# The first step of a batched Fourier transform: opposite rows folded by VectorE, products on 32x32 parts of TensorE

## The chip, the cores and the metric

The kernel runs on one core of a Trainium2 chip. The metric is the device time of one execution in microseconds (us). Each stated time is a median over runs; each profile is one execution recorded by the hardware profiler. The engines are called PE (TensorE, with PEld for its weight loads), DVE (VectorE), ACT (ScalarE), POOL (GpSimd) and SP (SyncE, which here only issues DMAs).

## The reference

Input is x with 8 batches of 3008 rows by 256 channels, in fp32. Along the 3008 rows each channel is Fourier transformed, multiplied by a complex filter, and transformed back; then a feed-forward block follows.

```python
X = np.fft.rfft(x, axis=1)
y = np.fft.irfft(X * (filt_r + 1j * filt_i), n=3008, axis=1)
h = y.reshape(8 * 3008, 256)
g = h @ w_gate                       # 256 x 1536
out = (g / (1 + np.exp(-g)) * (h @ w_val)) @ w_out   # 1536 x 256
```

## The kernel before

3008 is 47 x 64. A transform is done in steps of matrix products: the first is a discrete transform of length 47 over the rows that lie 64 apart, and later steps handle the 64 columns. The input is real, so half the spectrum is kept: NS = 24 of the 47 frequencies, each as a cosine and a sine row, 48 rows.

The main loop runs over the 8 batches `b`. In each batch 12 groups follow one another, 4 chunks of rows by 3 parts of the hidden dimension. A group is called a step, and a step takes some 27.6 us of PE when only the feed-forward block and little else is in it. In each step the program walks one list of 174 tokens, SCHEDULE, written by hand. A token names one piece of work: P, Q, A, B, E are products of the feed-forward block, and f, c, x, s, m, e, l, h, v and others are the ACT, DVE and POOL operations that feed them or take their results out of PSUM. Every instruction is put down in the order of this walk on its engine's queue (`pin` keeps it), so an engine never does a later one first.

The transform of batch b+1 is laid into the steps of batch b. The tokens b0 to b7 advance a generator of the step: in steps 0 to 3 `nxt.quads(g)`, the first step of the transform in four parts g, in steps 4 to 10 `nxt.fours(w)`, the later steps. This holds from batch 2's transform on, thus for six transforms; batches 0 and 1 are transformed in another way (`stage1` and on), and the first batch's steps are busy with preparing tables and weights as well.

`quads(g)` takes two pieces u of x. In SBUF a piece is a tile with 47 rows on partitions 0 to 46 (columns n) and 47 on partitions 64 to 110 (columns n + 32), loaded by `load_x` straight from x. At b0 PE makes eight products from these with the table `quad` (47 x 64, of which 48 columns are used), on four 64x64 quarters of its array, into four PSUM banks `wqa`. At b1 and b2 ACT copies the bank of one half and DVE adds and subtracts the bank of the other half. At b3 and b4 ACT's queue stores 48 rows to the DRAM tile `d`, and `load_x(u + 2)` asks for later pieces. At b5 and b6 of part 3 the filter and the first load of `fours`, `load_four(0)`, are asked for.

All SBUF tiles of the transform are rooms in one tile, `lent`, cut into 14 units of 512 floats per partition; `room_of` gives a letter's place (x the four units from 0, y and g two each after them, then e, t and tb). The first two loads of x for a transform, `following.load_x`, stand in step 11 of the batch before it, at tokens Q2 and B01. The weights of the feed-forward block are loaded anew for each step, in four pieces on SP's queue (`reload_weights`).

Names in the profile: `wk`, `wa` and `we` are PSUM banks of the gate and value products of the feed-forward block; `x`, `D`, `f`, `c`, `m` are SBUF operands made from them; `wA`, `wF` and `wG` are banks of the output product and `o` its sum in SBUF. DVE writes some operands into PSUM ahead of the products that add to them: `wa<-wk,f` (L1097), `wa<-wk,D` (L1097) and `we<-wk,c` (L335); PE can't start these products sooner.

Of the kernel before, what the change touches and what calls it, by code (L numbers as in the profile page):

```python
# [69 lines left out]
NV = 2  # L70
# [55 lines left out]
def dft_tables():  # L126
    n1, n2 = np.arange(N1), np.arange(N2)
    s, q = np.arange(NS), np.arange(NQ)
    ph = 2 * np.pi * (np.outer(n1, s) % N1) / N1
    w = np.stack([np.cos(ph), -np.sin(ph)], 1)  # L130
    wf = np.zeros((N1, 2, NS, 2, 2))
    wi = np.zeros((NS, 2, 2, N1, 2))

    v = np.stack([2 * np.cos(ph), -2 * np.sin(ph)], 0)
    v[0, :, 0], v[1, :, 0] = 1.0, 0.0
    for h in range(2):
        wf[:, h, :, :, h] = w.transpose(0, 2, 1)
# [24 lines left out]
    for tile_, first in zip(BACK, BACK_AT):  # L162
        for i, (n, row, a, rows) in enumerate(tile_):
            if n >= NH:
                back[row:row + rows, first + N1 * i:first + N1 * (i + 1)] = one_hi[a:a + rows]

    quad = np.zeros((128, 64))
    for h, turn in enumerate((ph, ph + 2 * np.pi * s / (2 * N1))):
        cols = np.stack([np.cos(turn), -np.sin(turn)], 2).reshape(N1, 2 * NS)
        quad[64 * h:64 * h + N1, 0:2 * NS] = cols  # L170
# [35 lines left out]
def kernel(  # L206
# [60 lines left out]
    def weights_of(b, k, g):  # L267
        return wt_1 if b == 0 and k < NT and g == 1 else wt_t

    dram_tiles = [wdpool.tile([2 * NS, N2, C], FP32, name=f"d{1 + i % 2}_{i // 2}")  # L270
                  for i in range(4)]
    yt_dram = [wdpool.tile([128, 3 * len(PAIRS), TQ], FP32, name=f"yt_{k}") for k in range(NT)]
    y_dram = [wdpool.tile([128, 8, TQ], FP32, name=f"y_{k}") for k in range(NCHUNK)]
    o_dram = [wdpool.tile([128, 4 * NH, RP], FP32, name=f"o_{k}") for k in range(NT)]
# [39 lines left out]

    def negated_filter(w, stage):

        t = room_of("et"[w % 2])[0:64].rearrange("p (s c) -> p s c", c=C)
# [282 lines left out]
    class Spectral:  # L600


        def __init__(self, b):
            self.b = b
            self.d1, self.d2 = [dram_tiles[2 * (b % 2) + i] for i in range(2)]
            self.d1_rows = self.d1.rearrange("a (h n) c -> (a h) n c", h=2)

# [21 lines left out]
        def load_x(self, u):  # L629
# [4 lines left out]
                        self.load(out=x0[u][r, a:a + n, :],  # L634
                                  in_=rows[r, 8 * u + a:8 * u + a + n, :])
            elif self.b > 1:
                if u < N_QUAD:
                    self.x[u] = room_of("x", u).rearrange("p (n c) -> p n c", c=C)
                    rows = x[self.b].rearrange("(r n) c -> r n c", n=N2)
                    for h in range(2):  # L640
                        for a, e in ((0, 32), (32, N1)):
                            self.load(out=self.x[u][64 * h + a:64 * h + e],
                                      in_=rows[a:e, 32 * h + 4 * u:32 * h + 4 * u + 4])
            elif u < N_ONE:
                self.x[u] = xpool.tile([NR, NV, C], FP32, name=f"x_{self.b}_{u}", tag="x")
                rows = x[self.b].rearrange("(r n) c -> r n c", n=32)
# [52 lines left out]
        def bank(self, name):  # L699
# [2 lines left out]
                return bank(name).rearrange("p (i c) -> p i c", i=NV)  # L702
            return fbank(name)

        def quads(self, g):

            pieces = (2 * g, 2 * g + 1)
            banks = {}
            for u in pieces:
                xt = self.x.pop(u)  # L710
                for h in range(2):
                    banks[u, h] = bank(f"qa_{self.b}_{u}_{h}")
                for cp in range(2):
                    for h in range(2):
                        r = slice(64 * h, 64 * h + N1)
                        pin(nc.tensor.matmul(  # L716
                            out=banks[u, h][64 * cp:64 * cp + 64], lhsT=quad_t[0][r, 0:64],
                            rhs=xt[r, 2 * cp:2 * cp + 2].rearrange("p n c -> p (n c)"),
                            start=True, stop=True))
            yield  # L720
            t1 = {u: room_of("yg"[i]).rearrange("p (n h c) -> p n h c", h=2, c=C)
                  for i, u in enumerate(pieces)}
            for u in pieces:
# [5 lines left out]
            d1 = self.d1.rearrange("a (n h) c -> a n h c", h=2)  # L729
            for u in pieces:  # L730
                for cp in range(2):
                    n = 4 * u + 2 * cp
                    pin(nc.scalar.dma_start(out=d1[:, n:n + 2], in_=t1[u][64 * cp:64 * cp + 2 * NS]))
                self.load_x(u + 2)
                yield
            if g == 3:
                self.load_filter(0)
                self.load_turns(0)
            yield
            if g == 3:  # L740
                self.load_four(0)

        def load_four(self, w):

            if w < N_FOUR:
                t = self.t2[w] = room_of("t").rearrange("p (s h c) -> p s h c", h=2, c=C)
                d1 = self.d1.rearrange("(s r) (n h) c -> s (r n) (h c)", r=2, h=2)
                for p in range(2):
                    s = 4 * w + 2 * p
                    self.load(out=t[64 * p:64 * p + 64].rearrange("p s h c -> p s (h c)"),  # L750
                              in_=d1[s:s + 2].rearrange("s q c -> q s c"))

        def load_filter(self, w):

# [626 lines left out]
    for b in range(B):  # L1381
# [10 lines left out]
        if b and nxt:  # L1392
            for n in range(N_QUAD // 2):
                bursts[n] = nxt.quads(n)
            for n in range(N_FOUR + 1):
                bursts[N_QUAD // 2 + n] = nxt.fours(n)
        bursts = [iter(p) for p in bursts]
        two = []
        for u in range(N_TWO + 2) if b == 0 else ():
# [18 lines left out]
        for step in range(NCHUNK * NG + (b == B - 1)):  # L1418
# [16 lines left out]
            for place, token in enumerate(SCHEDULE):  # L1435
# [31 lines left out]
                    continue  # L1467
                if b == 0 and (step, op) == (5, "A23"):
                    nxt.load_two(0)
                if b + 2 < B and (step, op) in ((11, "Q2"), (11, "B01")):  # L1470
                    following.load_x(int(op == "B01"))
                if b == 1 and step < 4 and op in FILTER_AT:
                    n = FILTER_AT.index(op)
                    if n < 4 and step < 3:
# [48 lines left out]
```

## Time and profile before

| | us |
|---|---|
| median of 3 runs (lowest, highest) | 2822.13 (2820.03, 2825.05) |
| profiled execution, its own time | 2823.7 |
| its span in the profile | 2821.6 |
| PE busy in it | 2787.5 |
| a step with `quads` (steps 0 to 2, step 3) | 29.2, 27.6 |
| a step with `fours` | 27.6 |

The mean granted TensorE clock was 0.997. The span runs from the first to the last recorded instruction; the execution's own time has 2.1 us more around it. "Busy" of PE counts matmuls that overlap one another once. An idle time is put beside the instruction that ended it, with the engine that released it.

### The profile page before, as it was taken

The numbers are of one execution on the slowest core, as the hardware profiler recorded it, in microseconds if no ns is written. First come the engines' busy times: TensorE is split into PE (matmuls) and PEld (weight loads), VectorE is DVE, ScalarE is ACT, GpSimd is POOL, SyncE is SP. The second block draws the span as 40 slices with busy tenths as digits, with TensorE's granted clock in tenths as the row PEclk, the third lists the DMA queues.
The fourth block names the chain that finished last, engine by engine and source line by source line (L and its number), as shares of the span: only waits on it lengthen the run. The fifth ranks groups of instructions, "written<-read, shape, count | busy, mean of one in ns | idle before, by whom it ended". The sixth has DMA issues, their size and how long they took to land.

```text
span 2821.6 us, 48540 instructions
## 1 busy us (share of the span) xinstructions
PE 2787.5 (99%) x15444; PEld 2319.9 (82%) x15444; DVE 1999.1 (71%) x4579; ACT 1564.7 (55%) x4176; POOL 1579.9 (56%) x1689
## 2 busy tenths in 40 slices
PE   8999999999999999999999999999999999999998
PEld 6877888888888888788888888878888888888887
DVE  7898767767667766667766677667676767666666
ACT  5675455555555555555555555555555555555554
POOL 4786576465545565456653566445655455545544
PEclk9999999999999999999999999999999999999999
DMA  9687876877666775667666676667766677654443
GB/s 214 224 272 237 283 242 211 285 233 232 181 188 207 246 221 175 204 215 229 222 185 197 211 246 201 188 190 236 228 205 181 213 224 227 192 153 148 153 137 82
DMA packets 362933, 586.59 MB, mean 208 GB/s; under 512 B 198620, under 2 KB 245660, under 8 KB 362536
## 3 DMA queue, kind: packets, MB, share of 16 engines
q1 hardware_dynamic: 337722, 533.61, 60.8%
q10 hardware_dynamic: 22318, 44.38, 5.7%
q0 software_dynamic: 2640, 5.51, 0.7%
q8 instruction: 125, 2.05, 0.3%
q14 instruction: 128, 1.05, 0.1%
HBM read 467.48 MB, written 101.34 MB: 202 GB/s over the span
## 4 chain that ended last, share of the span: by engine, by line
PE 91%; POOL 2%; DVE 2%; DMA 1%; issue 1%; ACT 1%; ACTq 0%; SPq 0%; POOLq 0%; DVEq 0%
PE wa L1075 25%; PE wk L1075 17%; PE wA L1172 16%; PE we L1075 13%; PE wG L1172 8%; PE wF L1172 4%; PE pd L978 3%; PE wqa L716 2%; PE wqc L775 1%; PE wqb L787 1%; POOL out_dram L1157 0%; POOL h L331 0%; PE pa L857 0%; DMA lent<-later_tbl 0%; PE pd L981 0%
## 5 line engine op out<-in xcount | busy, mean ns | idle before, releaser
L1075 PE MATMUL wa<-y_t,wt_t 128*128 128x188 f32 x4464 | 881.6, 324 | 4.0 <-DVE wa L1097 2.3
L1075 PEld LDWEIGHTS wa<-y_t,wt_t 128*128 128x128 f32 x4464 | 749.8, 191 | 79.5 <-ACT wa L1101 9.3
L1075 PEld LDWEIGHTS wk<-y,wt_t 128*128 128x128 f32 x2976 | 495.0, 190 | 109.5 <-issue 33.4
L1075 PE MATMUL wk<-y,wt_t 128*128 128x188 f32 x2976 | 572.0, 325 | 3.2 <-ACT f L1090 3.2
L331 POOL TENSOR_TENSOR h<-h 128x376 f32<-128x376 f32 x572 | 559.6, 1000 | 15.4 <-DVE h L328 15.2
L328 POOL TENSOR_TENSOR h<-h 128x376 f32<-128x376 f32 x190 | 182.8, 983 | 685.5 <-DVE h L1122 685.5
L1172 PE MATMUL wA<-h,wo_t 128*128 128x376 f32 x1532 | 551.8, 482 | 3.9 <-DVE o L328 2.1
L1075 PE MATMUL we<-y_t,wt_t 128*128 128x188 f32 x2232 | 431.7, 323 | 1.6 <-ACT we L1106 1.5
L331 POOL TENSOR_TENSOR D<-f,f 128x376 f32<-128x376 f32 x288 | 280.0, 986 | 258.4 <-ACT f L1090 256.0
L331 DVE TENSOR_TENSOR we<-we,m 128x376 f32<-128x376 f32 x576 | 319.8, 556 | 141.1 <-PE we L1075 73.9
L1075 PEld LDWEIGHTS we<-y_t,wt_t 128*128 128x128 f32 x2232 | 369.3, 190 | 2.7 <-ACT we L1106 2.1
L1172 PEld LDWEIGHTS wA<-h,wo_t 128*128 128x128 f32 x1532 | 274.9, 190 | 113.7 <-issue 7.0
L1110 ACT COPY m<-wa 128x376 f32<-128x376 f32 x576 | 272.7, 473 | 102.0 <-PE wa L1075 98.8
L335 DVE SCALAR_TENSOR_TENSOR y<-wk,c 128x376 f32<-128x376 f32 x480 | 244.8, 541 | 63.8 <-ACT c L1094 37.8
L1117 ACT ACTIVATE g<-wa 128x188 f32<-128x188 f32 x576 | 187.5, 326 | 164.7 <-PE wa L1075 154.9
L1117 ACT ACTIVATE u<-we 128x188 f32<-128x188 f32 x576 | 188.7, 328 | 160.2 <-DVE we L331 153.3
L1172 PE MATMUL wG<-h,wo_t 128*128 128x376 f32 x768 | 274.0, 479 | 0.0
L1094 ACT COPY c<-wk 128x376 f32<-128x376 f32 x288 | 136.5, 474 | 226.0 <-PE wk L1075 196.7
L1090 ACT ACTIVATE f<-wk 128x376 f32<-128x376 f32 x288 | 140.4, 488 | 168.6 <-PE wk L1075 118.0
L1106 ACT COPY we<-y 128x376 f32<-128x376 f32 x480 | 222.3, 480 | 19.8 <-DVE h L1122 14.4
L1122 DVE TENSOR_TENSOR h<-wa,g 128x188 f32<-128x188 f32 x576 | 199.4, 347 | 38.0 <-ACT g L1117 37.6
L1122 DVE TENSOR_TENSOR h<-we,u 128x188 f32<-128x188 f32 x576 | 198.5, 345 | 28.8 <-ACT u L1117 17.3
(193 smaller groups left out, 3523.0 us busy)
## 6 DMA issues: line engine op xcount, KB each, us to landing
wt_t<-w_all SPq DMA_DIRECT2D x174, 896.0 KB
wt_t<-w_all SPq DMA_DIRECT2D x174, 768.0 KB
lent<-filter SPq DMA_DIRECT2D x36, 1024.0 KB
lent<-d SPq DMA_DIRECT2D x84, 256.0 KB
d<-lent ACTq DMA_DIRECT2D x84, 256.0 KB
d<-lent ACTq DMA_DIRECT2D x96, 192.0 KB
lent<-raw SPq DMA_DIRECT2D x144, 128.0 KB
t<-d SPq DMA_DIRECT2D x114, 128.0 KB
```

The lines of the kernel that those rows point to most:

```text
L328: return eng.tensor_tensor(out=dst, in0=a, in1=b, op=ALU.add)
L331: return eng.tensor_tensor(out=dst, in0=a, in1=b, op=ALU.subtract)
L335: return nc.vector.scalar_tensor_tensor(out=dst, in0=a, scalar=-1.0, in1=b, op0=ALU.mult, op1=ALU.subtract)
L978: pin(nc.tensor.matmul(out=rows, lhsT=self.t4[k, i][:, j, ts(cb, 128)], rhs=cols, start=j == 0, stop=True, skip_group_check=True))
L1075: pin(nc.tensor.matmul(out=ps[:, z], lhsT=self.wt[:, SLOT[p], z], rhs=rhs, start=start and z == 0, stop=True, skip_group_check=True))
L1090: pin(act.mul(self.small(f"f{i}", f"f{i}", 1), t[f"k{i}"], -1.0))
L1094: pin(act.copy(out=self.small(f"c{i}", f"c{i}", 1), in_=t[f"k{i}"]))
L1106: pin(act.copy(out=self.bank(f"e{at}"), in_=t[f"y{at}"]))
L1110: pin(act.copy(out=self.small(f"m{at}", "m", 4), in_=t[f"a{at}"]))
L1117: pin(act.activation(out=self.small(op, "g", 3, 1)[:, 0], in_=ps[:, 1], func=AF.Silu))
L1122: pin(v.tensor_tensor(out=dst, in0=ps[:, 0], in1=g, op=ALU.mult))
L1172: pin(nc.tensor.matmul(out=self.tiles[at], lhsT=wo_t[:, JB * q + i, WO[p], :], rhs=self.hs[i][:, HID[p]], start=start and i == 0, stop=Tru ...
```

## The change

Rows a and 47 - a of a discrete transform of length 47 share their cosine and have opposite sines. The changed kernel uses this. `fold(g)` lets DVE add and subtract 128x512 tiles `up` and `down` (four operations for each part g), and the products at b0 are 24 rows by 32 columns, with a cosine table for sums and a sine table for differences: sixteen of them for a part, on sixteen 32x32 parts of PE's array, into the same four banks. A part's pieces are now g and g + 4. The two halves of the frequencies (even and odd turns) stand in separate 32-row blocks, so 64 rows are stored for each piece, unmixed, to a new DRAM tile `quads_dram`.

`down` needs the rows in falling order. `turn_rows`, called in step 8 at token Q0 of the batch two before, copies them from x to the DRAM tile `turned`, with a negative stride, by six DMAs on SP's queue. `load_x(g)` then loads one `down` tile of 128 x 1024 (from `turned`) and four `up` blocks of 32 x 1024. `load_x(0)` stands in step 11 at Q0; `load_x(g + 1)` follows the fold's last operation at b7. `first_fold` does the fold of part 0 at b4 to b7 of step 11; the fold of part g + 1 runs at b4 to b7 of part g's own step. `load_four` reads the new layout by four DMAs in place of two. The table `quad` and the room of `negated_filter` (batch 1 only) are changed to suit.

On each engine this comes to, over the program: PE 192 products of 64x512 replaced by 384 of 32x512; DVE 96 operations added; SP 192 loads of x replaced by 24 and 96, with 36 copies and 72 issues of `load_four` added; ACT 96 stores of 192 KB replaced by 96 of 256 KB.

```diff
+            self.quads_dram, self.turned = quads_dram[b % 2], turned_dram[b % 2]
...
-                if u < N_QUAD:
-                    self.x[u] = room_of("x", u).rearrange("p (n c) -> p n c", c=C)
+                if u < N_QUAD // 2:
+                    self.x[u] = [room_of("x", n) for n in range(2)]
+                    up, down = self.x[u]
+                    at = self.turned.rearrange("(g q) p c -> g p q c", q=4)[u]
+                    self.load(out=down.rearrange("p (q c) -> p q c", c=C), in_=at)
                     rows = x[self.b].rearrange("(r n) c -> r n c", n=N2)
-                    for h in range(2):
-                        for a, e in ((0, 32), (32, N1)):
-                            self.load(out=self.x[u][64 * h + a:64 * h + e],
-                                      in_=rows[a:e, 32 * h + 4 * u:32 * h + 4 * u + 4])
+                    for n in range(4):
+                        first = 16 * n + 4 * u
+                        self.load(out=up[ts(n, 32)].rearrange("p (q c) -> p q c", c=C),
+                                  in_=rows[0:32, first:first + 4])
...
+        def turn_rows(self):
+            xb, to = x[self.b], self.turned
+            end = NS if self.b > 3 else 32
+            for h in range(2):
+                for i in range(2):
+                    n, p = 32 * h + 16 * i, 1 - h
+                    lane = 64 * h + 32 * i
+                    self.load(out=to[:, lane + p:lane + end],
+                              in_=bass.AP(tensor=xb.tensor, ap=[[C, 16], [-N2 * C, end - p], [1, C]],
+                                          offset=xb.offset + ((N1 - 1) * N2 + n) * C))
+                    if h == 0:
+                        self.load(out=to[:, lane], in_=xb[n:n + 16])
+
+        def fold(self, g):
+            if g < N_QUAD // 2:
+                up, down = self.x.pop(g)
+                self.x[g] = [room_of("e"), room_of("t")]
+                for t, f in zip(self.x[g], (add, sub)):
+                    for half in range(2):
+                        a = ts(half, NV * C)
+                        pin(f(nc.vector, t[:, a], up[:, a], down[:, a]))
+                        if t is self.x[g][1] and half:
+                            self.load_x(g + 1)
+                        yield
+
+        def first_fold(self):
+            for _ in range(4):
+                yield
+            yield from self.fold(0)
+
         def quads(self, g):
-            pieces = (2 * g, 2 * g + 1)
...
+            pieces = (g, g + N_QUAD // 2)
+            banks = {(u, h): bank(f"qa_{self.b}_{u}_{h}") for u in pieces for h in range(2)}
+            parts = self.x.pop(g)
+            for cp in range(2):
+                for t in range(2):
+                    for i, u in enumerate(pieces):
+                        for h in range(2):
+                            r, c = 32 * (2 * h + i), 32 * (2 * cp + t)
+                            pin(nc.tensor.matmul(
+                                out=banks[u, h][c:c + 32], lhsT=quad_t[0][r:r + NS, ts(t, 32)],
+                                rhs=parts[t][r:r + NS, ts(cp, NV * C)],
+                                start=True, stop=True))
+            yield
+            fold = self.fold(g + 1)
...
-                    pin(nc.scalar.dma_start(out=d1[:, n:n + 2], in_=t1[u][64 * cp:64 * cp + 2 * NS]))
-                self.load_x(u + 2)
+                    pin(nc.scalar.dma_start(out=d1[:, n:n + 2], in_=t1[u][64 * cp:64 * cp + 64]))
+                if u == pieces[1]:
+                    next(fold, None)
                 yield
             if g == 3:
                 self.load_filter(0)
                 self.load_turns(0)
+            next(fold, None)
             yield
             if g == 3:
                 self.load_four(0)
+            next(fold, None)
+            yield
+            next(fold, None)
...
-                    self.load(out=t[64 * p:64 * p + 64].rearrange("p s h c -> p s (h c)"),
-                              in_=d1[s:s + 2].rearrange("s q c -> q s c"))
+                    for r in range(2):
+                        a = 64 * p + 32 * r
+                        self.load(out=t[a:a + 32].rearrange("p s h c -> p s (h c)"),
+                                  in_=d1[r, :, s:s + 2])
...
+        if b + 2 < B:
+            bursts[-1] = following.first_fold()
...
-                if b + 2 < B and (step, op) in ((11, "Q2"), (11, "B01")):
-                    following.load_x(int(op == "B01"))
+                if b + 2 < B and (step, op) == (8, "Q0"):
+                    following.turn_rows()
+                if b + 2 < B and (step, op) == (11, "Q0"):
+                    following.load_x(0)
```

More of the change, by code (lines that the diff above doesn't have):

```diff
@@ L165, in dft_tables @@
                 back[row:row + rows, first + N1 * i:first + N1 * (i + 1)] = one_hi[a:a + rows]
[L167 to L170, printed above, removed]
+    quad = np.zeros((4, 32, 2, 32))
+    for h in range(2):
+        turn = 2 * np.pi * (np.outer(2 * n1[0:NS] + h, s) % (2 * N1)) / (2 * N1)
+        quad[2 * h:2 * h + 2, 0:NS, 0, 0:NS], quad[2 * h:2 * h + 2, 0:NS, 1, 0:NS] = np.cos(turn), -np.sin(turn)
+        quad[2 * h:2 * h + 2, 23 * h] *= np.array([0.5, 0.0])[:, None]
+    quad = quad.reshape(128, 64)
     four = np.zeros((128, N_FOUR + 1, 2, 4, 64))
@@ L271 @@
                   for i in range(4)]
+    quads_dram = [wdpool.tile([64, N2, C], FP32, name=f"quads_{i}") for i in range(2)]
+    turned_dram = [wdpool.tile([16, 128, C], FP32, name=f"turned_{i}") for i in range(2)]
     yt_dram = [wdpool.tile([128, 3 * len(PAIRS), TQ], FP32, name=f"yt_{k}") for k in range(NT)]
@@ L315, in negated_filter @@
     def negated_filter(w, stage):
-        t = room_of("et"[w % 2])[0:64].rearrange("p (s c) -> p s c", c=C)
+        t = lent[64 * (w % 2):64 * (w % 2) + 64, 12 * NV * C:14 * NV * C]
+        t = t.rearrange("p (s c) -> p s c", c=C)
         if stage == 0:
@@ L703, in bank @@
             return fbank(name)
-        def quads(self, g):
-            pieces = (2 * g, 2 * g + 1)
[L708 to L719, printed above, removed]
+        def turn_rows(self):
[10 more added lines that the diff above has]
+                        self.load(out=to[:, lane], in_=xb[n:n + 16])
@@ new lines, in first_fold @@
+        def first_fold(self):
+            for _ in range(4):
+                yield
+            yield from self.fold(0)
+        def quads(self, g):
+            pieces = (g, g + N_QUAD // 2)
[4 more added lines that the diff above has]
+                    for i, u in enumerate(pieces):
+                        for h in range(2):
+                            r, c = 32 * (2 * h + i), 32 * (2 * cp + t)
[3 more added lines that the diff above has]
+                                start=True, stop=True))
@@ L728, in quads @@
                 yield
-            d1 = self.d1.rearrange("a (n h) c -> a n h c", h=2)
+            d1 = self.quads_dram.rearrange("a (n h) c -> a n (h c)", h=2)
             for u in pieces:
@@ L746, in load_four @@
                 t = self.t2[w] = room_of("t").rearrange("p (s h c) -> p s h c", h=2, c=C)
-                d1 = self.d1.rearrange("(s r) (n h) c -> s (r n) (h c)", r=2, h=2)
+                d1 = self.quads_dram.rearrange("(r s) (n h) c -> r n s (h c)", r=2, h=2)
                 for p in range(2):
                     s = 4 * w + 2 * p
-                    self.load(out=t[64 * p:64 * p + 64].rearrange("p s h c -> p s (h c)"),
-                              in_=d1[s:s + 2].rearrange("s q c -> q s c"))
+                    for r in range(2):
+                        a = 64 * p + 32 * r
+                        self.load(out=t[a:a + 32].rearrange("p s h c -> p s (h c)"),
+                                  in_=d1[r, :, s:s + 2])
         def load_filter(self, w):
```

## The prediction

> **What bounds the kernel now.** The page comes first: the busy line, the slices of the span, and the summary of the chain that ended last.
>
> ```profile
> PE 2787.5 (99%) x15444; PEld 2319.9 (82%) x15444; DVE 1999.1 (71%) x4579; ACT 1564.7 (55%) x4176; POOL 1579.9 (56%) x1689
> PE   8999999999999999999999999999999999999998
> PEclk9999999999999999999999999999999999999999
> DMA  9687876877666775667666676667766677654443
> PE 91%; POOL 2%; DVE 2%; DMA 1%; issue 1%; ACT 1%; ACTq 0%; SPq 0%; POOLq 0%; DVEq 0%
> ```
>
> TensorE (PE) is busy in every slice and makes up 91% of the chain; only work taken from PE, or a wait given to it, moves the end. The groups by form price what is exchanged (busy us and mean ns stand ahead of the last bar):
>
> ```profile
> L716 PE MATMUL wqa<-lent,quad 47*64 47x512 f32 x384 | 46.7, 602 | 0.0
> L725 ACT COPY lent<-wqa 128x512 f32<-128x512 f32 x48 | 28.1, 586 | 47.0 <-PE wqa L716 47.0
> L845 DVE TENSOR_TENSOR lent<-lent 128x512 f32<-128x512 f32 x24 | 16.4, 683 | 0.0
> ```
>
> The first step is 24 bursts (6 transforms, batches 2 to 7, four each) and 46.7 us of PE in all, so no PE saving here can exceed 1.7%. L845 is the nearest row to the new VectorE (DVE) additions. The timeline of one burst tells what stands behind it (start, duration):
>
> ```profile
> 2150.96 1.95 PE L716 MATMUL wqa<-lent,quad 47*64 47x512 f32 x16
> ...
> 2152.10 0.59 ACT L725 COPY lent<-wqa 128x512 f32<-128x512 f32 x1 [1.75 <-PE wqa L716]
> 2152.72 0.69 DVE L331 TENSOR_TENSOR lent<-lent,wqa 128x512 f32<-128x512 f32 x1 [3.00 <-ACT lent L725]
> ...
> 2155.82 0.55 DVE L1097 SCALAR_TENSOR_TENSOR wa<-wk,f 128x376 f32<-128x376 f32 x1
> 2156.28 0.54 DVE L328 TENSOR_TENSOR o<-o,wA 128x376 f32<-128x376 f32 x1
> 2156.73 0.67 PEld L1075 LDWEIGHTS wa<-y_t,wt_t 128*128 128x128 f32 x4
> ```
>
> DVE waits 3.00 us for the ACT copy, runs four tied operations (to 2155.45), then x and wa. The wa it writes ends at 2156.37, and PE takes it up at 2156.73: a slack of .36 us.
>
> **What the Trainium skill says.** "TensorEngine Tiling (Array Packing)", PSUM Bottleneck: tiling speeds up TensorE, "not PSUM evacuation". The trace agrees: a copy of .586 and four operations .6 to .7 apart follow a 1.95 us burst. "TensorE: Matmul & The Clock Gate", Measured speedup vs the span model: 16 tiles of 32x32 span one matmul plus some 4 ns for each further tile. The trace shows four 64x64 tiles together, 7 ns apart; sixteen it does not show. "VectorE: DVE Perf Modes", the section on the errata of SBUF sources: an fp32 add of 512 takes 691 ns; the row above has 683.
>
> **The change part by part.** *PE.* Each burst goes from 8 products of 47x64 tiles to 16 of 24x32, each in two passes of .427 us. Before: four rounds of passes, 1.88 us from first start to the next PE start, and 1.97 with the switch into it. After, if all 16 tiles run together: .05 + 2 x .427 + 15 x .007 + .09 (drain at the end, from the same gap) = 1.10. The saving is .77 us, that is 24 x .77 = 18.5 us if PE were alone.
>
> It is not alone. Before, the first bank was ready 1.09 us after the start; after, by the same terms, at 1.17. So the ACT copy starts .08 later while PE is through .77 earlier and comes for wa. Of the slack .36 there remain .36 - .08 - .03 (wake-up) = **.24 us gained per burst**; the other .53 becomes a wait of PE on `wa<-wk,f`.
>
> *DVE.* 96 fold operations are added, four per burst. The fold of part g+1 stands at tokens b4 to b7 of burst g, that of part 0 at b4 to b7 of step 11 of the batch before. One occupies DVE .604 us (start to start in a row). In the first step:
>
> ```profile
> 2158.63 0.55 DVE L1097 SCALAR_TENSOR_TENSOR wa<-wk,D 128x376 f32<-128x376 f32 x1
> ...
> 2159.90 0.51 PEld L1075 LDWEIGHTS wa<-y_t,wt_t 128*128 128x128 f32 x3
> ```
>
> The b4 fold falls between the two o additions, ahead of this wa, which has 2159.90 - 2159.18 = .72 to spare: .12 remains, so the .24 shrinks to .12. b5 and b6 fall into idle DVE. Ahead of b7:
>
> ```profile
> 2168.58 0.55 DVE L335 SCALAR_TENSOR_TENSOR we<-wk,c 128x376 f32<-128x376 f32 x1
> ...
> 2169.59 0.67 PEld L1075 LDWEIGHTS we<-y_t,wt_t 128*128 128x128 f32 x4
> ```
>
> .46 to spare against .604 + .03: .17 lost. Net of step 0: .12 - .17 = -.05. The same reading of the timeline of the other steps, from the DVE write to PE's weight load that takes it: step 1 has 1.28 to spare at b7, so +.24; step 2 has .82 at b4 and .48 at b7, so .24 - .15 = +.09; step 3 has no folds, +.24. Step 11's b7 has 1.28: 0. Sum .52 a transform, x 6 = **3.1 us gained**. DVE is busy 18.9 to 21.6 us of a step of 29.2 (step 3: 27.6); 2.4 more leaves idle time. Should every fold reach PE, the bound is 96 x .604 = 58 us. POOL gets no instruction; it is 11 to 19 us busy per step, and that idle time covers operations lengthened by DVE's traffic.
>
> *Loads.* 192 SP loads of x (128 and 60 KB) become 24 of 512 KB in 1 KB rows plus 96 of 128 KB. They are issued at step 11 Q0 and at each b7, there behind the fold's last operation, so SP waits for DVE; the weight reloads of pieces 2 and 3 stand behind that wait, needed only steps' ends later. In step 11 before batch 6's transform SP comes to them at 2119.7; the queue still moves 768 KB of weights until 2122.9; 512 rows of 1 KB (1.75 us by the packets of like loads in this trace, an estimate) and 128 of 4 KB (2 us) end at about 2126.8, the fold is due at 2126.3, and PE would feel it only from 2128.3: 0, with 1.5 us of margin. In batch 1, with DMA at .77 to .82, they land 1 to 3 us ahead of need: 0.5 us lost, taken within 0 to 2. ACT's 96 stores grow from 192 to 256 KB (+6 MB of 587) and load_four goes from two SP issues to four: 0, since DMA is .64 to .73 busy in these steps; without that cover, 6 MB at the mean 208 GB/s is 29 us.
>
> *Turned copies.* Six DRAM to DRAM copies per transform at step 8 Q0, on SP's queue. From batch 1 on they fill 3 us in which the queues are idle, and delay the next loads to about 3 us ahead of need: 0. For batch 2 they fall in batch 0, in a busy place (columns: PE, PEld, DVE, ACT, POOL busy, clock, DMA share, GB/s; then, from PE's waits of that stretch, us in total, times, longest):
>
> ```profile
> 324.00:336.00 12.00, 11.38 (x56) 9.11 (x55) 8.07 (x17) 4.72 (x12) 9.87 (x13) 1.00 0.91 294
> 336.00:348.00 12.00, 11.22 (x57) 9.29 (x56) 10.57 (x23) 5.92 (x16) 11.92 (x14) 1.00 0.97 322
> ```
>
> ```profile
> PE pb L897 <- DMA lent<-d: 1.5, 2, 1.1
> ```
>
> The DMA engines are full, and PE already waits there for `lent<-d`. 2048 packets of 1 KB, at the 46 ns that a packet takes in the filter's DRAM to DRAM copies of this trace, over 16 engines are 5.9 us; holes of 1.3 us take some. I charge **4.6 us, once**; bounds 2 (other work absorbs it) and 9.4 (5.9 plus six SP issues of .58).
>
> *Sum.* -3.1 + .5 + 4.6 = +2.0 on the profiled 2823.7 (span 2821.6 and 2.1 around it). That run is 1.6 above the median, so 2824.1 in the median's terms.
>
> **Rivals.**
> Main case (.60): as above. With its bounds (batch 0 at 2 to 9.4, gain 0 to 7) 2817 to 2833.
> A, PE's saving goes through (.11): 2822 - 18.5 + 4.6 + .5 = 2809, or 2804 if the copies hide too. For it: PE is 91% of the chain. Against it: the slack of .36. It decides if the chain of copy, four operations and wa starts .5 us earlier.
> B, slower by the DMA ring (.22): the large loads and turned copies land late, and DVE, in order, stands at the b4 fold. Place: step 11 and steps 0 to 2. Price: us for us behind the 1.5 us margin; .5 late in each of 24 loads is 12 us, with the 4.6 of batch 0 some 2836 (2830 to 2842). For it: the .97 row; against it: shares of .64 to .73 later.
> C, the change doesn't do what it says (.05): at most four of the small tiles run together, as four do now. Then four groups of two passes, 3.5 us a burst, 24 x 1.55 = 37 us: 2860. For it: no run here shows sixteen; against it: the skill's span.
> Rest .02.
>
> **Numbers.** 0.2%, 5.6 us, is about what a measurement of this kernel can tell from no change. Main case: .03 faster, .43 same, .14 slower. With A, B, C and the rest: faster .14, same .43, slower .43. The range 2810 to 2842 leaves out the lower part of A (.08) and C, with tails of B and the main case.
>
> **What would show it.** Right: a burst near 1.1 us; a new PE wait on wa behind DVE of about .5 us x 24; gaps at b7 of steps 0 and 2; PE busy some 13 to 18 us less with more waits; `pb<-lent` at about 340 us waiting 5 us or so longer. Wrong: a burst of 1.9 us or more; folds waiting for `lent<-turned`; the wait on wa missing and the time near 2805.

## The result, and the profile after

The changed kernel takes 2848.72 us in the median of 4 runs (2846.08 to 2850.18); the kernel before takes 2821.45 beside it. The ratio is 1.0094, with a 95% interval of 1.0076 to 1.0111: slower by 27 us, above the range of 2810 to 2842 us. The page of the kernel after, its busy line, PE's slices and the chain that ended last:

```profile
PE 2789.1 (98%) x15828; PEld 2316.2 (81%) x15828; DVE 2053.2 (72%) x4675; ACT 1554.3 (55%) x4176; POOL 1580.9 (55%) x1689
...
PE   8999899899999999999999999999999999999998
...
PE 79%; DVE 2%; POOL 1%; issue 1%; ACT 1%; DMA 1%; SPq 0%; ACTq 0%; DVEq 0%; POOLq 0%
```

Two slices of PE that were 9 are 8: the fifth and eighth, each 71 us long (285 to 356 us, 498 to 570 us). The loss is local. The groups by form of the kernel after, for the rows that the change touches:

```profile
L333 DVE TENSOR_TENSOR lent<-lent 128x512 f32<-128x512 f32 x48 | 39.0, 812 | 25.2 <-DMA lent<-in_x_dram 25.2
L336 DVE TENSOR_TENSOR lent<-lent 128x512 f32<-128x512 f32 x48 | 35.0, 729 | 0.0
...
L757 PE MATMUL wqa<-lent,quad 24*32 24x512 f32 x768 | 27.4, 600 | 0.0
L767 ACT COPY lent<-wqa 128x512 f32<-128x512 f32 x48 | 25.8, 589 | 46.1 <-PE wqa L757 46.1
```

The products fell from 46.7 to 27.4 us, 19.3 in all, so PE's part of the change works. (PE's busy time in all still rose by 1.6 us; passes that run at a lower granted clock, told below, count as busy.) The 96 folds (L333 and L336) take 74.0 us of VectorE, and it stood idle 25.2 us ahead of them, waiting for loads of x.

Where the time went is read most sharply by laying the matmuls of both traces side by side, those of the first step left out, and noting how much later each starts than its twin before. The table gives the change of this shift in us within each stage, for the kernel after and for the runs told below: the start (to 300 us, where, e7 and e8 apart, nothing of the change is at work yet, and the traces still lie between -5.0 and +1.8), batch 0's step 8 with the end of step 7, its steps 9 and 10 (s9+), its step 11, batch 1's steps 0 to 3 (b1 s0+), and the five later transforms together. Each row is one profiled execution:

```
                     start   b0 s8  b0 s9+  b0 s11  b1 s0+   later
kernel after          -1.1    +8.6    +0.8    +1.6   +16.0    +1.5
e1  pool copies       -3.4    +7.2    +4.2    +0.1   +17.0    +3.8
e2  SP stores         -2.0    +9.6    +1.0    +1.6    -1.2    +1.2
e3  no folds          -0.1    +8.5    +1.3     0.0    -0.3    +6.3
e4  late evacuation   -1.3   +11.5    +1.2    +0.4   +15.9    +8.9
e5  no copies         -4.7    +1.0     0.0    +0.6   +16.1    +2.0
e6  tiny copies       -5.0    +5.1    +1.0    +0.7   +16.7    +1.1
e7  early copies      +2.8    -0.5     0.0    +0.4    -1.2    +3.3
e8  POOL folds        +0.5     0.0     0.0     0.0    -1.3    +1.1
e9  split, POOL       -1.5    +1.6     0.0     0.0    -3.2    +7.5
e10 all SP stores     -1.4    +0.9    +6.6    +0.3    -1.3    -1.8
e11 split, VectorE    -3.5    +0.9    +6.3    +1.7    -2.6    +8.1
e12 both, POOL        +1.8    +1.0     0.0     0.0    -3.2   -11.1
e13 before, edits     +1.4    +0.8     0.0     0.0    -1.5    -0.6
e14 both, VectorE     -4.4    +1.0     0.0    +1.6    -2.6    -7.9
```

Of the kernel after's 27.4 us (its start was 1.1 us ahead), 16.0 fell in steps 0 to 3 of batch 1, 9.4 in steps 8 to 10 of batch 0, 1.6 in step 11. After batch 1 each transform loses a further .3 us.

A caution on the twin: the trace of before has two waits of PE for ACT's f of its own, in batch 1's step 3 (at 545 us) and in batch 3's step 2 (at 1198 us). All runs lack them, e13 too, and so the table shows some 1.5 us in "b1 s0+" and .6 in "later" as gains that the change did not make. Without them batch 1 loses 17.5 us, and a later transform .4.

**Batch 1.** In its steps 1 and 2 PE loses 7.8 and 9.0 us. The waits of the kernel after between 440 and 545 us (of SP's queue, then of DVE and PE from 478 on; us in total, times, longest):

```profile
SPq L624 <- DMA quads<-lent: 31.4, 3, 15.9
...
DVE lent L333 <- DMA lent<-in_x_dram: 14.4, 2, 7.6
...
PE wa L1124 <- DVE wa L1146: 12.1, 4, 5.9
```

From bottom to top: PE waits for wa from VectorE; VectorE stands at the b4 fold and waits for x; and SP, which should have asked for that x, stands behind a store `quads<-lent`. That is a store of the next burst, of other data. The timeline of SP's queue shows the five loads of one part:

```profile
478.17 0.39 SPq L624 DMA_DIRECT2D lent<-turned  x1
478.61 19.00 SPq L624 DMA_DIRECT2D lent<-in_x_dram  x4
```

The third of the four goes out at 495.57; SP was through with the second at 479.7. The trace gives the semaphore of each DMA: it waits for semaphore 108, and ACT's store issued at 492.52 raises 108 when it lands. In the trace the DMAs of SP and ACT together use eight such completion semaphores in turn, and this load goes out only when the DMA that had its semaphore before has landed. The turns were dealt with the store ahead of the load; on the chip SP comes to the load 13 us before ACT comes to the store. The DMA engines were not in the way while SP stood (columns as in the prediction: the last three are clock, DMA share and GB/s):

```profile
484.00:490.00 6.00, 6.00 (x58) 4.13 (x56) 3.38 (x9) 2.92 (x7) 3.01 (x4) 1.00 0.02 3
```

Only after SP's release did all that had queued up fill them: the fourth load, issued at 495.93, took 6.3 us to land.

The two long waits of PE, 5.7 and 5.9 us, are not the whole of the 16.8 us. During each the granted clock fell to .50, and it stayed there for 3.8 and 4.9 us after PE had work again. After the first:

```profile
504.77:508.53 3.76, 3.76 (x10) 3.34 (x11) 2.45 (x7) 0.80 (x2) 3.73 (x6) 0.50 0.96 373
```

Passes of wa then start .31 us apart in place of .16; by the matmuls' shifts that adds 1.9 and 2.5 us to the two waits.

**Step 8 of batch 0.** SP's queue, then PE's wait between 300 and 420 us, then the window just behind that wait:

```profile
332.26 4.08 SPq L624 DMA_DIRECT2D turned<-in_x_dram  x6
...
337.65 0.48 SPq L589 DMA_DIRECT2D back<-back_tbl  x1
345.08 0.32 SPq L1354 DMA_DIRECT2D y<-y  x1
```

```profile
PE pb L946 <- DMA lent<-d: 9.5, 1, 9.5
```

```profile
354.94:358.34 3.40, 3.40 (x9) 3.03 (x10) 1.29 (x2) 0.00 (x0) 0.00 (x0) 0.50 1.02 402
```

SP stands still from 338.1 to 345.1 us. Its next load, y<-y, waits for semaphore 103, whose turn before belongs to a store of ACT's queue issued at 341.04. PE then waits 9.5 us, from 345.5 to 354.9, for a load `lent<-d` that SP asks for at 351.55, behind all that it had put off. The granted clock is .50 from 348.1 to 358.3 us, so within the wait and 3.4 us beyond it; that adds 1.7 us.

**Step 11 of batch 0.** Here SP issued the loads of x one behind another (427.4 to 429.9 us), with the DMA share at .97 from 428 to 432 us. VectorE stood 2.8 us at the b4 fold, and PE waited 1.1 us for the wa behind it. The loss is gone where VectorE has no folds (e3, e8, e9, e12).

**The burst.** The timeline of the burst of the prediction, in the kernel after:

```profile
2177.79 1.14 PE L757 MATMUL wqa<-lent,quad 24*32 24x512 f32 x32
...
2179.06 1.07 ACT L767 COPY lent<-wqa 128x512 f32<-128x512 f32 x2 [1.89 <-PE wqa L757]
...
2181.12 2.85 ACTq L775 DMA_DIRECT2D quads<-lent  x4
...
2182.79 0.55 DVE L1146 SCALAR_TENSOR_TENSOR wa<-wk,f 128x376 f32<-128x376 f32 x1
...
2183.45 0.62 PEld L1124 LDWEIGHTS wa<-y_t,wt_t 128*128 128x128 f32 x4 [0.60 <-POOL h L336]
...
2184.02 0.47 ACT L1143 COPY c<-wk 128x376 f32<-128x376 f32 x1 [3.49 <-DVE o L333]
```

From first start to PE's next start it takes 1.07 us, before 1.88: sixteen tiles run together, .81 us saved. PE's weight loads then stand idle .60 us ahead of wa, whose operand VectorE ends writing at 2183.34 (the name behind the arrow is another: POOL's h of that moment ends at 2183.46, after the weight load has begun, so it is not what was waited for). The accounts of the first step of this transform, from the matmuls' shifts: -.81 by the burst; +.07 at wk and wA behind ACT's copy; +.57 at wa; +.14 at the next wk behind ACT's f; +.22 at we behind the b7 fold; in all +.20. Steps 1, 2 and 3 come to -.22, +.54 and +.07.

### The profile page after: what moved, and what is told of

The parts are those of the page before. It is cut to its first block, busy times and chain, and to the rows that moved or that the text cites. A ratio compares the mean times of both kernels' runs of the same rounds, so it can differ in the third digit from the quotient of the medians.

```text
span 2848.4 us, 49286 instructions
## 1 busy us (share of the span) xinstructions
PE 2789.1 (98%) x15828; PEld 2316.2 (81%) x15828; DVE 2053.2 (72%) x4675; ACT 1554.3 (55%) x4176; POOL 1580.9 (55%) x1689
## 4 chain that ended last, share of the span: by engine, by line
PE 79%; DVE 2%; POOL 1%; issue 1%; ACT 1%; DMA 1%; SPq 0%; ACTq 0%; DVEq 0%; POOLq 0%
PE wa L1124 23%; PE wA L1221 14%; PE wk L1124 13%; PE we L1124 11%; PE wG L1221 7%; PE wF L1221 4%; PE pd L1027 3%; PE wqc L824 1%; PE wqb L836 1%; PE wqa L757 1%; POOL h L336 1%; DVE lent L336 1%; POOL D L336 0%; ACT lent L767 0%; DVE wa L1146 0%
## 5 line engine op out<-in xcount | busy, mean ns | idle before, releaser
L1124 PE MATMUL wk<-y,wt_t 128*128 128x188 f32 x2976 | 580.2, 327 | 0.6 <-ACT f L1139 0.2
L336 POOL TENSOR_TENSOR h<-h 128x376 f32<-128x376 f32 x572 | 559.6, 998 | 15.4 <-DVE h L333 15.2
L333 POOL TENSOR_TENSOR h<-h 128x376 f32<-128x376 f32 x190 | 182.9, 983 | 679.9 <-DVE h L1171 679.9
L336 POOL TENSOR_TENSOR D<-f,f 128x376 f32<-128x376 f32 x288 | 280.6, 987 | 278.4 <-ACT f L1139 260.7
L336 DVE TENSOR_TENSOR we<-we,m 128x376 f32<-128x376 f32 x576 | 318.9, 555 | 125.2 <-PE we L1124 60.6
```

The source lines that it names most:

```text
L333: return eng.tensor_tensor(out=dst, in0=a, in1=b, op=ALU.add)
L336: return eng.tensor_tensor(out=dst, in0=a, in1=b, op=ALU.subtract)
L1124: pin(nc.tensor.matmul(out=ps[:, z], lhsT=self.wt[:, SLOT[p], z], rhs=rhs, start=start and z == 0, stop=True, skip_group_check=True))
```

## The experiments

Two theories stood against each other for the 27 us. S: the turns of the completion semaphores hold SP back. D: the DMA engines are full, and the added bytes take their time. All medians are beside the kernel before in the same session (2820.1 to 2821.4). Edits are to the changed kernel unless said otherwise.

**e1: batch 2's copies on POOL's queue.**

```diff
+            def put(**kw):
+                pin((nc.gpsimd if self.b == 2 else nc.sync).dma_start(**kw))
...
-                    self.load(out=to[:, lane + p:lane + end],
+                    put(out=to[:, lane + p:lane + end],
...
```

> The changed kernel, with the six turned copies of batch 2's transform (step 8 of batch 0) issued on POOL's queue in place of SP's; the same bytes at the same place, and nothing else is altered. Theory S (semaphore turns): the 9.4 us lost in step 8 of batch 0 come from SP standing still from 338.1 to 345.1 us, because its load y<-y has the completion semaphore (103) that an ACT store issued only at 341.04 had the turn before; six DMAs fewer among those of SP and ACT shift the turns, and that wait goes. Then step 8 loses at most 3 us and the whole is some 2841 us. Rival D (DMA share): 2048 packets of 1 KB take 5.9 us from engines that are full; the bytes are still there, so step 8 still loses 6 to 9 us and the whole stays at 2846 to 2850. On both, batch 1 still loses 15 us in steps 1 and 2.

2850.54 us, ratio 1.0099 (1.0082 to 1.0116): no better. POOL came to the copies at 313.8 us, 18 us ahead of SP, so they moved as well; around them PE lost 7.2 and then 4.2 us. SP no longer stood ahead of y<-y (it went out at 338.78), and PE lost no less: S in the form that the 7 us of SP's standing are the loss fell here. As the copies moved, the run says nothing for or against D.

**e2: batch 1's stores on SP's queue.**

```diff
-                    pin(nc.scalar.dma_start(out=d1[:, n:n + 2], ...))
+                    queue = nc.sync if self.b == 2 else nc.scalar
+                    pin(queue.dma_start(out=d1[:, n:n + 2], ...))
```

> The changed kernel, with the 16 stores of the first step in batch 1 (batch 2's transform) issued on SP's queue in place of ACT's; bytes, folds and loads are as they were. Theory S: in steps 0 and 1 of batch 1 SP's third load of x stands 15.8 and 13.9 us behind an ACT store of the next burst whose completion semaphore it shares; with all these DMAs on one queue their turns follow SP's own order, so the loads go out at once and the 7.8 and 8.3 us that PE lost in steps 1 and 2 of batch 1 go: some 2833 us. Rival D: the loads are late because the filter's DMAs fill the engines (share .77 to .82); the bytes are the same and SP has 16 issues more, so 2847 to 2851.

2832.05 us, ratio 1.0036 (1.0023 to 1.0050): 16.7 less. SP's timeline, then PE's waits from 476 to 545 us, in this kernel:

```profile
477.97 0.39 SPq L624 DMA_DIRECT2D lent<-turned  x1
478.41 2.05 SPq L624 DMA_DIRECT2D lent<-in_x_dram  x4
```

```profile
PE wa L1125 <- DVE wa L1147: 0.5, 2, 0.2
```

The four loads take 2.05 us to issue in place of 19.00. The DMA share tells against D too; step 1 of batch 1 in the kernel after, then in this one:

```profile
478.80:516.00 37.20, 31.22 (x180) 25.44 (x181) 21.60 (x49) 18.31 (x46) 18.96 (x24) 0.91 0.71 234
```

```profile
478.80:508.00 29.20, 28.95 (x180) 23.71 (x179) 21.28 (x49) 18.62 (x46) 18.46 (x24) 1.00 0.91 277
```

Nearly the same bytes (8.7 MB in the kernel after, 8.1 here, rate times time) pass in 8 us less, at a share of .91 in place of .71. In batch 1 it was semaphore turns.

**e3: no folds.** The fold operations are left out, and the next load stands at b3:

```diff
-                        pin(f(nc.vector, t[:, a], up[:, a], down[:, a]))
...
+                if u == pieces[0]:
+                    self.load_x(g + 1)
```

> The changed kernel without the 96 fold operations: the products read the loaded rows themselves, so sums and differences are left out of the computation, and load_x(g+1) is asked for at b3, after the products, as before the change. Theory: the folds cost in two ways, by the deadline that they give the loads (batch 1, some 15 us) and by their time on VectorE. What is left per later transform is the saving of PE (.81 a burst) less its wait for wa behind the evacuation (about .5 a burst): a gain of .2 to .25 a burst, -0.8 to -1.0 us per transform where the changed kernel has +.3. Step 8 of batch 0 still loses 9. In all 2825 to 2831 us. Rival: the folds' time on VectorE costs nothing and the rest is as in the changed kernel, then the later transforms stay at +.3 each and only batch 1 gets better, 2831 to 2835.

2838.48 us, ratio 1.0059 (1.0044 to 1.0074), worse than expected. Batch 1's loss went, which agrees with the loads' deadline. But later transforms lose 6.3 together, not gain: the load of turned rows now has the semaphore that ACT's fourth store needs next, that store waits, and so do c, m and f behind it on ACT. PE waits for `ACT f` 5.6 us in batches 3 to 6. As a price for the folds the run is spoiled.

**e4: the second piece's evacuation at b3.**

```diff
+                if u == pieces[1]:
+                    yield
                 pin(nc.scalar.copy(out=t1[u][:, :, 0], in_=low))
                 pin(sub(nc.vector, ...))
                 pin(add(nc.vector, ...))
-                yield
+                if u == pieces[0]:
+                    yield
```

> The changed kernel, with the evacuation of a burst's second piece (ACT copy, subtraction and addition) put at token b3 in place of b2, behind the DVE operation that writes wa<-wk,f. Theory (evacuation chain): PE's wait of about .5 us on this wa in each burst goes, since two operations of .66 us no longer stand ahead of it; but the same operations and the b4 fold now stand ahead of wa<-wk,D, with .1 to .7 us to spare, so PE gets some of it back later: 0 to .4 us better a burst, 2839 to 2849. Rival: the two PSUM banks held longer stop a later product of the step, then each burst is slower by .5 or more, 2858 and up.

2859.72 us, ratio 1.0136 (1.0121 to 1.0151): the rival, with its reason. The wait on wa is gone; in batches 3 to 6 PE waits 3.5 us for `ACT lent`, the copy that frees a bank for wA, and 5.4 for `ACT f`.

**e5: no copies for batch 2, and e6: six tiny DMAs in their place.** In both, batch 2's down tiles are loaded as rising rows, and batch 4's copies carry up to 32 rows in place of 24.

```diff
-                    following.turn_rows()
+                    if b:
+                        following.turn_rows()
+                    else:                          # e6 alone
+                        for i in range(6):
+                            pin(nc.sync.dma_start(out=turned_dram[0][:, i], in_=x[2][16 * i:16 * i + 16]))
...
```

> The changed kernel without the six turned copies of batch 2's transform; its down tiles are loaded straight from x in rising order, with packets of 1 KB as before, so the reversal of rows is left out for that batch alone. On both theories step 8 of batch 0 loses nothing (+9.4 in the changed kernel): 2838 to 2841 us. If it keeps 3 us or more, the loss in batch 0 is neither the copies' bytes nor their issues.

> As the kernel without batch 2's turned copies, but six DMAs of 16 packets each stand in step 8 of batch 0 where the copies stood: the issues and the turns of the completion semaphores are there, the 2 MB are not. Rival D (the copies' bytes on full DMA engines): as without copies, within 2 us, 2838 to 2842. Theory S (issues and semaphore turns): step 8 still loses 5 us or more, 2844 to 2849.

2843.74 and 2843.73 us, ratios 1.0076 (1.0059 to 1.0093) and 1.0076 (1.0060 to 1.0093). The medians can't part them, since the start scatters; the stages can. PE's wait in step 8, of e5 and of e6:

```profile
PE pb L948 <- DMA lent<-d: 2.3, 3, 1.3
```

```profile
PE pb L948 <- DMA lent<-d: 5.5, 2, 5.3
```

Steps 8 to 10 lose 1.0 without copies, 6.1 with six tiny ones, 9.4 with the copies. So of 8.4 us some 5 come with six more issues of .63 us on SP and the turns they shift, and some 3 with the 2 MB. Neither S nor D alone. The turns differ, too: in e6 SP doesn't stand 7 us ahead of y<-y, but 3.4 us for the semaphore of a weight load. The split is rough, since kernels with no copy in step 8 or 9 lie between -.5 and +1.6 there. e5's median is some 3 us above its expectation; its four runs lie between 2837.8 and 2844.7.

**e7: copies earlier, at step 6 Q0, and e2's stores.**

```diff
-                if b + 2 < B and (step, op) == (8, "Q0"):
+                if b + 2 < B and (step, op) == ((8, "Q0") if b else (6, "Q0")):
```

> The changed kernel with two edits: batch 1's first-step stores on SP's queue (which gave 2832), and batch 2's turned copies at Q0 of step 6 of batch 0 in place of step 8, where the DMA share before was .50 (242 to 260 us) and not .91 to .97. If the loss in step 8 was the bytes meeting full engines, most of 9.4 us goes: 2823 to 2827. If the six DMAs cost the same wherever they stand: 2830 to 2834.

2826.85 us, ratio 1.0018 (1.0012 to 1.0025), as expected. The copies still cost 4.9 us where they now stand (in the table's start).

**e8: folds on POOL**, with e7's edits: `f(nc.gpsimd, ...)` in place of `f(nc.vector, ...)`.

> As the kernel with SP stores and early copies, and the folds on POOL in place of VectorE (its 128x512 addition takes 1.28 us in L845's POOL row). Theory (VectorE's time is what folds cost in steps 0 and 2): the waits of PE on we at b7 go and a little of PE's saving remains, -.2 to -.5 a transform in place of +.3: 1 to 4 us below the kernel with early copies. Rival: four operations of 1.28 us stand ahead of POOL's D and h operations in its order, and PE waits for those: .5 to 2 us a step more, 10 to 40 us above it.

2825.42 us, ratio 1.0013 (1.0006 to 1.0019). Both missed: no harm by POOL, but the later transforms still lose .2 each. The folds' time on VectorE was not the main thing that held PE's saving back.

**e9: POOL folds, e2's stores, copies at step 10, and the evacuation split**: as e4, but the ACT copy stays ahead of the new `yield`.

> The kernel with SP stores in batch 1 and folds on POOL, with two further edits that lie in different stages: batch 2's turned copies at Q0 of step 10 of batch 0 (DMA share .62 in 397 to 412 us before), and of a burst's second piece only the DVE subtraction and addition at b3, behind wa<-wk,f; its ACT copy, which frees a PSUM bank, stays at b2. Theory (PE waits on wa because two DVE operations of the second piece stand ahead of it): the .5 us wait goes in each burst, and later transforms change from +.2 to between -.5 and -1.5 us each. Rival (what holds PE after the burst is as much ACT, by f, c and m behind its four store issues of some 2.9 us): the wait moves to wk behind f and the transforms stay within .3 of +.2. Copies: 0 to 2 us lost in place of 4.9. In all 2812 to 2823 by the first, 2819 to 2825 by the rival.

2824.87 us, ratio 1.0020 (1.0013 to 1.0028). The later transforms lose 1.5 each, more than either side gave; that the total falls into the rival's range is chance. PE's waits from 900 to 2600 us, and ACT in the first step of batch 6:

```profile
PE wk L1128 <- ACT f L1143: 11.5, 13, 0.9
```

```profile
2157.23 3.33 ACTq L779 DMA_DIRECT2D quads<-lent  x4
...
2162.12 0.54 ACT L1143 ACTIVATE f<-wk 128x376 f32<-128x376 f32 x1
```

The wait on wa is gone from the list; PE waits for f, which ACT reaches late because four stores hold its queue 3.33 us, 1.1 of it a wait for VectorE's moved operations. The copies at step 10 cost nothing that stands out.

**e10: POOL folds, all first-step stores on SP, no split; copies at A23 of step 9.**

> The kernel with folds on POOL, with the first step's stores on SP's queue in all six transforms, and batch 2's turned copies at A23 of step 9 of batch 0. Theory (ACT's four store issues, 2.9 us a burst, delay its f, c and m, and that takes back the last .1 of each burst): with them off ACT each later transform gains .2 to .5, so from +.2 to between 0 and -.3. Rival: ACT's issues hide behind its idle time, and nothing changes by more than .1 a transform; or SP, now waiting on DVE at b3 and b4, holds back the weight reloads behind it, and steps lose .5 us or more. In all 2818 to 2824.

2824.93 us, ratio 1.0015 (1.0008 to 1.0022). Later transforms gain .4 each (1.8 together; .24 without before's own wait, as the theory had it) where e8 lost .2: the last wait, on f, is gone, that on wa stays. The copies at this place cost 6.6, which puts the total just above its range.

**e11: the split and e2's stores with folds on VectorE, copies as in e10.**

> The kernel with SP stores in batch 1 and folds on VectorE as in the changed kernel; the second piece's subtraction and addition at b3 behind wa<-wk,f, its ACT copy at b2; batch 2's copies at A23 of step 9 of batch 0. Theory: as with POOL folds the wait on wa goes, but the b4 fold and the two moved operations now stand ahead of wa<-wk,D, which has .1 to .7 us to spare: from +.3 to between +.2 and -.6 a transform. If folds on VectorE cost nothing, the transforms come out as with the folds on POOL. In all 2816 to 2825.

2833.10 us, ratio 1.0044 (1.0029 to 1.0059): missed, and for e9's reason, the wait on f.

**e12: both, the split and all stores on SP**, with POOL folds and copies at step 10.

> The kernel with folds on POOL, copies at Q0 of step 10, the second piece's subtraction and addition behind wa<-wk,f, and the first step's stores on SP in all six transforms. Theory (two chains take PE's saving back: the evacuation on VectorE ahead of wa, and behind it ACT's four store issues ahead of f; each edit alone only uncovers the other): with both away a burst keeps .5 to .6 of the .81 us, -1.6 to -2.4 a transform, in all 2808 to 2814. Rival (a third wait stands just behind, or SP's waits at b3 and b4 hold its weight reloads back): -.5 a transform or less, 2818 to 2824.

2806.80 us, ratio .9952 (.9938 to .9966): faster than the kernel before by 13 us, and than the changed kernel by 42. Each later transform gains 2.2 (2.1 without before's own wait), as forecast; the total lies 1 us under its range. The burst's stage:

```profile
2145.34 0.55 DVE L1149 SCALAR_TENSOR_TENSOR wa<-wk,f 128x376 f32<-128x376 f32 x1
...
2146.42 0.47 ACT L1146 COPY c<-wk 128x376 f32<-128x376 f32 x1 [2.02 <-PE wk L1127]
...
2146.70 0.67 PEld L1127 LDWEIGHTS wa<-y_t,wt_t 128*128 128x128 f32 x4
```

wa ends at 2145.89, .81 us ahead of PE, and c no longer waits for stores. From 900 to 2600 us PE has no listed wait at all.

**e13: the kernel before with the same two edits, and e14: e12 with folds on VectorE.**

> The kernel before the change, with the two edits that freed its saving afterwards: the first step's stores on SP's queue in all six transforms, and the second piece's subtraction and addition at b3, behind wa<-wk,f. Theory (the gain of the last kernel comes from PE's shorter burst, which the edits only let through): the old burst of 1.88 us leaves PE no wait on wa or wk, so nothing is there to be freed; within 3 us of before, 2817 to 2824, later transforms within .3 of 0. Rival (the edits are worth their 10 us by themselves): 2806 to 2814.

> The kernel that ran in 2806.8, with the folds back on VectorE. Theory (folds on VectorE cost where a PSUM write stands behind them: we at b7 in steps 0 and 2, and wa<-wk,D behind the b4 fold): PE loses .2 to .4 us in each of steps 0 and 2 and nothing in steps 1 and 3, so later transforms come out at -1.2 to -1.8 in place of -2.1: 2808 to 2813. Rival (VectorE's idle time takes the folds): -2.0 to -2.2, within 1 us of 2806.8.

e13 took 2819.71 us, ratio .9995 (.9987 to 1.0004): the edits alone bring nothing clear of noise. (Its trace lacks before's two waits for f, as its stores are off ACT.) e14 took 2813.14, ratio .9972 (.9960 to .9984), its later transforms gaining 1.6 each in place of 2.2: that is the folds' time on VectorE, .6 us a transform. In its batch 6 it is lost in step 0 (.49) and step 2 (.32), at wa<-wk,D and at we.

## Why the prediction was wrong

The main case had the loss at 2.0 us and it was 27. The step that failed is that of the loads in batch 1; the others were off by less. Step by step:

- *PE's burst*: forecast 1.10 us and a saving of .77; measured 1.07 and .81. Rival C fell. But the sign "PE busy some 13 to 18 us less" did not come: it rose by 1.6.
- *Evacuation*: the step was right in kind. PE's shift at wa was forecast at .53 and came at .41 to .50, with .07 to .10 more behind it. (.36 - .08 - .03 is .25, not .24, which changes nothing.) The term was short in two ways: each wait of PE is followed by a second delay of about .10 at the next pass, and wk's wait behind ACT's copy and f, which the prediction set to nothing, takes .1 to .3. A burst was to keep .24 us ahead of the folds' cost; in step 1, where folds cost nothing, it kept .22, in step 3 -.07.
- *Folds*: steps 0 and 2 were forecast at -.17 and -.15 by b7. In step 0 it was .22 and in step 2 .31, with .27 more at the wa behind it, and together with the rest the four steps of batch 6 came to +.59 us (on average +.3 a transform) in place of -.52. Over five later transforms this is a miss of 4 to 5 us.
- *Loads in batch 1*: "0.5 us lost, taken within 0 to 2" is the step that failed; it was 16.0, with e2's edit -1.2. The prediction looked at the ring's bytes and at SP's order, and not at what a DMA waits for before it is issued. The loads' time between b7 and b4 is short, and a store of the next burst could stand ahead of them by its semaphore. In the trace of before this could be seen: SP stands 9.0 us ahead of a load of x at 485.70, whose semaphore ACT's store of 481.97 had before; there the load was not due for longer.
- *Clock*: the prediction had no term for it. The granted clock of .50 in and behind the three long waits adds some 6 us to what the waits themselves cost, and is within the 16.0 and the 9.4.
- *Step 11*: forecast 0, measured 1.6, by loads that landed late on full engines.
- *Turned copies*: forecast 4.6, bounds 2 to 9.4; measured 9.4. That it meets the upper bound is chance: without copies 1.0 is lost too (e5), of the rest issues and turns are more than half (e6), and 1.7 is the clock.
- *Rival B* had the right place, VectorE standing at the b4 fold, and the wrong cause and price: not .5 us in each of 24 loads but some 8 us behind each of two, with the DMA engines at a share of .02 while SP stood. Its own cause, bytes, shows in step 11, for 1.6 us.
- *Rival A*, PE's saving going through, needed two more edits (e12), after which .5 us a burst go through.
- The statement of the Trainium skill, "TensorEngine Tiling (Array Packing)", PSUM Bottleneck, that tiling doesn't speed up evacuation, held here with its number: .81 us saved on PE, .57 us of it waited for the evacuation. That of "TensorE: Matmul & The Clock Gate", Measured speedup vs the span model, on the span of 16 tiles, held in form: the tiles of a pass start 7 ns apart, where the page has some 4, two passes of .427 us and 15 such starts make .96, and 1.07 from first start to the next product's start was measured.

What stays open: how the turns would fall with another order of the same DMAs was not tried beyond these kernels, and the part of step 8's loss that is the bytes' (some 3 us) rests on one trace each of three kernels.

## What to carry to other kernels

A load that is needed sooner is not safe because its bytes fit: see in the trace which semaphore it waits for before it is issued, and which DMA, of whichever queue, had that semaphore before. A saving on the busiest engine passes through only as far as the slack of each chain that follows it, and an edit that opens one chain can look worthless or harmful while the next is shut (e9, e10), so edits on two such chains are to be judged together. Lay two traces side by side by the starts of the same matmuls: it parts a loss of a tenth of a us from a scatter of several.

## What the hardware showed that was not expected

A wait of PE costs about .10 us more than itself: after the short waits of a burst the next pass of the same product starts a further .07 to .11 late (e9: +.23 at wk, then +.11; the kernel after: +.41 at wa, then +.11). Four stores of 256 KB on ACT's queue hold ACT 2.85 to 3.33 us in the bursts shown, the waits between them included, in which it computes nothing. And in PE's three long waits (9.5, 5.7 and 5.9 us) the granted clock fell to .50 within 2.6 to 4.0 us of the wait's start and stayed there 3.4 to 4.9 us beyond its end.
